# Infini-attention and GELU FFN on one core: four-head score visits, resident attention weights, one ring of PSUM banks, FFN in column halves, transposes by DMA

## The chip, the cores and the metric

The kernel runs on one core of a Trainium2 chip. TensorE does matmuls (PE in the profile; PEld is its load of the stationary operand), VectorE (DVE) and ScalarE (ACT) work elementwise and may read PSUM, where matmul results land, GpSimd (POOL) works elementwise on SBUF, and SyncE (SP) issues the DMAs. The metric is device time in microseconds (us): the median of several runs.

## The reference

One transformer layer on x of 2048 x 576, in bfloat16. Attention has 32 heads of 18 columns and goes through four segments of 512 rows. Within a segment it is causal softmax attention; beside it, a memory M, z, made of earlier segments' keys and values, is read by the queries, and a gate per head mixes both. Then follows an FFN of width 4608. Both have a layernorm before and a residual after.

```python
for s in range(N):
    logits = jnp.einsum('bhqd,bhkd->bhqk', qs, ks) * scale + mask
    a_dot = jnp.einsum('bhqk,bhkd->bhqd', _softmax(logits, axis=-1), vs)
    pq = phi(qs)                      # t + 1 where t > 0, else exp(t)
    a_mem = einsum(pq, M) / (einsum(pq, z)[..., None] + 1e-06)
    outs.append(g * a_mem + (1.0 - g) * a_dot)
    M = M + jnp.einsum('bhld,bhle->bhde', phi(ks), vs)
    z = z + jnp.einsum('bhld->bhd', phi(ks))
...
h = x + (o @ wo)                      # o from the layernormed x
h2 = h + gelu(_layernorm(h) @ w1 + b1) @ w2 + b2
```

## The kernel before

A segment s has four tiles of 128 rows and goes through four phases.

*Phase P* makes Q, K and V. Per tile: layernorm (`layernorm`, L175 to L184: statistics on DVE, a power on POOL, one DVE operation); five transposes on TensorE into PSUM (L195) and a copy by ScalarE to `xnT_t` (L66); three projections of ten matmuls each of 288 columns (`proj`, L203 and L205); ScalarE copies Q and K to padded tiles, 32 columns a head (L72); eight more TensorE transposes each for Q and K (L259, L264), which DVE copies to `QT_al_s` and `KT_al_s` (L260, L265); V goes to `v_augs` (L268), and phi(K) is made by ACT, POOL and DVE (L254, L270, L272). After four tiles, 32 small matmuls add up the memory (L281).

*Phase A* is attention, by groups of four heads. The scores come transposed, keys on partitions. There are three steps per group, of 512, 384 + 128 and 256 columns. In each step the four heads' scores go to two PSUM tiles of two banks (`unit2`, pool psS with two buffers; matmuls at L338, one head per 32 rows of TensorE); ScalarE takes the exp of a pair of heads at a time (L347), POOL clears what lies above the diagonal (L349), and TensorE multiplies with V into the bank `ox` (PV, L356), which DVE clears first (L308) and reads at the end (L361 to L371). From the second segment on, phi(Q) is made per group (L312 to L316: e_g on ACT, r_g on POOL, pq on DVE) and multiplied with the memory (L323).

*Phase B* projects the output and adds the residual. Per tile: five TensorE transposes of `o_nat`, copy, `proj` with wo, add of x (L392), layernorm, five transposes into `xn2T_s`; POOL adds b2 (L401) and the sum goes to the DRAM tile `hd` (L402).

*Phase C* is the FFN. F1: nine groups of four column tiles; a group's weights `w1g` are loaded by three DMAs (L410 to L414, two buffers); a column tile is five matmuls of 512 columns (L419, L420) in a bank of psC (three buffers), copied to `hT` by DVE (L424); gelu runs over twelve column tiles at once (L428). F2: per row tile and half of the columns 36 matmuls (L437) add up in a bank; DVE adds `hc`, loaded from `hd` (L432), and the output is stored (L441).

The code is traced as P, A, B of all four segments and then C of all four. A scheduler lays down each engine's order by priority, that is by order of tracing, and lets later work in where earlier work isn't ready. psS serves P, A and B; psC serves C alone. Buffers of a pool are handed out in the order of tracing, and a new user waits until the old one is done. All DMAs are issued on SP's queue, in order. The attention weights go through three buffers and are loaded anew for each segment; w2 is loaded once, in four chunks, behind the first segment's inputs.

Of the kernel before, what the change touches and what calls it, by code (L numbers as in the profile page):

```python
# [8 lines left out]
ACT = mybir.ActivationFunctionType  # L9
# [3 lines left out]
PSUM = bass.MemoryType.PSUM  # L13


@with_exitstack
def kernel(
# [15 lines left out]
    dbg = None  # L33
    nseg_run = None
# [11 lines left out]
    KT = 5  # L46
# [8 lines left out]
    FORCE4 = False  # L55
    HIPRI = True
    GB = 3
    EVAC_ACT = 0
    XT_DVE = False
    QK_DVE = False  # L60

    def copy_xt(out, in_):
        if XT_DVE:
            nc.vector.tensor_copy(out=out, in_=in_)
        else:
            nc.scalar.copy(out=out, in_=in_)  # L66

    def copy_qk(out, in_):
        if QK_DVE:
            nc.vector.tensor_copy(out=out, in_=in_)  # L70
        else:
            nc.scalar.copy(out=out, in_=in_)  # L72
    if nseg_run is None:
        nseg_run = NSEG
    SYNC_DEP = mybir.DependencyInfo(mybir.DependencyClass.Sync, mybir.DependencyReason.DATA)

    const = ctx.enter_context(tc.tile_pool(name="const", bufs=1))
    wpool = ctx.enter_context(tc.tile_pool(name="wpool", bufs=1))
    xpool = ctx.enter_context(tc.tile_pool(name="xpool", bufs=2))
    xtp = ctx.enter_context(tc.tile_pool(name="xtp", bufs=2))  # L80
    xn2Tp = ctx.enter_context(tc.tile_pool(name="xn2Tp", bufs=2))
    tmp1 = ctx.enter_context(tc.tile_pool(name="tmp1", bufs=1))
    alpool = ctx.enter_context(tc.tile_pool(name="alpool", bufs=1))
    ptpool = ctx.enter_context(tc.tile_pool(name="ptpool", bufs=2))
    ptpool1 = ctx.enter_context(tc.tile_pool(name="ptpool1", bufs=1))
    hpool = ctx.enter_context(tc.tile_pool(name="hpool", bufs=2))
    hbpool = ctx.enter_context(tc.tile_pool(name="hbpool", bufs=1))
    small = ctx.enter_context(tc.tile_pool(name="small", bufs=4))
    w1pool = ctx.enter_context(tc.tile_pool(name="w1pool", bufs=2))
    outpool = ctx.enter_context(tc.tile_pool(name="outpool", bufs=2))  # L90
    psS = ctx.enter_context(tc.tile_pool(name="psS", bufs=2, space=PSUM))
# [3 lines left out]
    x_pre = []  # L95
    for tl in range(TPS):
        xt = xpool.tile([P, D], BF16, tag="x", name="xt") if tl < 2 else None
        if xt is not None:
            nc.sync.dma_start(out=xt[:], in_=x[tl * P:(tl + 1) * P, :])
        x_pre.append(xt)  # L100

    def load_w(W, tag):
        wt = wpool.tile([P, KT, D], BF16, tag=tag, name="wt_" + tag)
        nc.sync.dma_start(out=wt[:, 0:4, :], in_=W[0:512, :].rearrange("(k p) n -> p k n", p=P))
        nc.sync.dma_start(out=wt[0:64, 4, :], in_=W[512:576, :])
        nc.gpsimd.memset(wt[64:KTAIL, 4, :], 0.0)
        return wt

    w_pre = {"wq": load_w(A_wq, "wq"), "wk": load_w(A_wk, "wk"), "wvo": load_w(A_wv, "wvo")}
# [28 lines left out]
    for j in range(2):  # L138
        nc.vector.memset(MZ_blk[j][:], 0.0)

    q_pads = [const.tile([P, H, 32], BF16, name=f"q_pad{j}") for j in range(2)]
    k_pads = [const.tile([P, H, 32], BF16, name=f"k_pad{j}") for j in range(2)]
    phik_pads = [const.tile([P, H, 32], BF16, name=f"phik_pad{j}") for j in range(TPS)]
    v_augs = [const.tile([P, H, Dh + 1], BF16, name=f"v_aug{j}") for j in range(TPS)]
    xn_bufs = [const.tile([P, XW], BF16, name=f"xn{j}") for j in range(2)]
    xn2_bufs = [const.tile([P, XW], BF16, name=f"xn2_{j}") for j in range(1)]
    o_nat = const.tile([P, TPS, XW], BF16, name="o_nat")
    for tx in xn_bufs:
        nc.gpsimd.memset(tx[:, D:XW], 0.0)
    for tpad in q_pads + k_pads:  # L150
        nc.gpsimd.memset(tpad[:, :, Dh:32], 0.0)
    for tpad in phik_pads:
        nc.vector.memset(tpad[:, :, Dh:32], 0.0)
    for tv in v_augs:
        nc.vector.memset(tv[:, :, Dh:Dh + 1], 1.0)
    for tx in xn2_bufs:
        nc.gpsimd.memset(tx[:, D:XW], 0.0)
        nc.gpsimd.memset(tx[:, D:D + 1], 1.0)
    nc.gpsimd.memset(o_nat[:, :, D:XW], 0.0)

    hd = tc.dram_tile([S, D], F32, name="hd")
    hT = const.tile([P, NF, L], BF16, name="hT")
    w2_sb = const.tile([P, NF, D], BF16, name="w2_sb")
    w2v = B_w2.rearrange("(f p) d -> p f d", p=P)
    late = {"x_last": None, "w2_last": None}

    def issue_w2():
        for c in range(4):
            d = nc.sync.dma_start(out=w2_sb[:, c * 9:(c + 1) * 9, :], in_=w2v[:, c * 9:(c + 1) * 9, :])
            if late["x_last"] is not None:  # L170
                tc.add_manual_dep(d.ins, late["x_last"].ins.name, SYNC_DEP, reason="bulk FFN weights after the first segment's inputs")
            late["w2_last"] = d

# [12 lines left out]
    def unit2():  # L186
        return psS.tile([P, 2, 512], F32, tag="st2", name="u2")

    def bf16v(bank_ap):
        return bank_ap.bitcast(BF16)  # L190

    def transposes5(src, bank_ap):
        pt = bf16v(bank_ap)[:, 0:KT * P].rearrange("p (k q) -> p k q", q=P)
        for k in range(KT):
            nc.tensor.transpose(out=pt[:, k, :], in_=src[:, k * P:(k + 1) * P], identity=ident[:])  # L195
        return pt

    def proj(xT_t, wt):
        u = unit2()
        for hf in range(2):  # L200
            ps = u[:, hf, :]
            for k in range(4):
                nc.tensor.matmul(out=ps[:, 0:HALF], lhsT=xT_t[:, k, :], rhs=wt[:, k, hf * HALF:(hf + 1) * HALF],  # L203
                                 start=(k == 0), stop=False)
            nc.tensor.matmul(out=ps[:, 0:HALF], lhsT=xT_t[0:KTAIL, 4, :], rhs=wt[0:KTAIL, 4, hf * HALF:(hf + 1) * HALF],  # L205
                             start=False, stop=True)
        return u

    def hview(u):
        return u[:, :, 0:HALF].rearrange("p b (h d) -> p b h d", d=Dh)  # L210

    def pad_view(tpad):
        return tpad[:, :, 0:Dh].rearrange("p (b h) d -> p b h d", b=2)

    st_P = {}
    st_B = {}

    def phase_P(s):
        if s == 0:
            wq_t, wk_t, wv_t = w_pre["wq"], w_pre["wk"], w_pre["wvo"]  # L220
        else:
            wq_t = load_w(A_wq, "wq")
            wk_t = load_w(A_wk, "wk")
            wv_t = load_w(A_wv, "wvo")
        QT_al_s = alpool.tile([P, G, L], BF16, tag="qt", name="QT_al_s")
        KT_al_s = alpool.tile([P, G, L], BF16, tag="kt", name="KT_al_s")
        for tl in range(TPS):
            t = s * TPS + tl
            cols = slice(tl * P, (tl + 1) * P)
            if s == 0 and x_pre[tl] is not None:  # L230
                xt = x_pre[tl]
            else:
                xt = xpool.tile([P, D], BF16, tag="x", name="xt")
                xd = nc.sync.dma_start(out=xt[:], in_=x[t * P:(t + 1) * P, :])
                if s == 0:
                    late["x_last"] = xd
                    if tl == TPS - 1:
                        issue_w2()
            xn = xn_bufs[tl % 2]
            layernorm(xt[:], xn)  # L240
            u0 = unit2()
            pt = transposes5(xn, u0[:, 0, :])
            xnT_t = xtp.tile([P, KT, P], BF16, tag="xnT", name="xnT_t")
            copy_xt(xnT_t[:], pt)
            uq = proj(xnT_t, wq_t)
            q_pad = q_pads[tl % 2]
            copy_qk(pad_view(q_pad), hview(uq))
            if dbg is not None and "q" in dbg:
                nc.sync.dma_start(out=dbg["q"][t * P:(t + 1) * P, :].rearrange("p (h d) -> p h d", d=Dh), in_=q_pad[:, :, 0:Dh])
            uk = proj(xnT_t, wk_t)  # L250
            k_pad = k_pads[tl % 2]
            copy_qk(pad_view(k_pad), hview(uk))
            ek = tmp1.tile([P, H, Dh], BF16, tag="e", name="ek")
            nc.scalar.activation(out=ek[:].rearrange("p (b h) d -> p b h d", b=2), in_=hview(uk), func=ACT.Exp)  # L254
            ut = unit2()
            ptq = bf16v(ut[:, 0, :]).rearrange("p (g q) -> p g q", q=P)
            q2d = q_pad[:].rearrange("p h d -> p (h d)")
            for g in range(G):
                nc.tensor.transpose(out=ptq[:, g, :], in_=q2d[:, g * P:(g + 1) * P], identity=ident[:])  # L259
            nc.vector.tensor_copy(out=QT_al_s[:, :, cols], in_=ptq)  # L260
            ptk = bf16v(ut[:, 1, :]).rearrange("p (g q) -> p g q", q=P)
            k2d = k_pad[:].rearrange("p h d -> p (h d)")
            for g in range(G):
                nc.tensor.transpose(out=ptk[:, g, :], in_=k2d[:, g * P:(g + 1) * P], identity=ident[:])  # L264
            nc.vector.tensor_scalar(out=KT_al_s[:, :, cols], in0=ptk, scalar1=maskcol[:], scalar2=None, op0=ALU.mult)  # L265
            uv = proj(xnT_t, wv_t)
            v_aug = v_augs[tl]
            nc.vector.tensor_copy(out=pad_view(v_aug), in_=hview(uv))  # L268
            rk = tmp1.tile([P, H, Dh], BF16, tag="r", name="rk")
# [228 lines left out]
```

## Time and profile before

The runs took 619.56 us in the median (619.19 to 621.7). One execution was profiled:

| | us | share of the span |
|---|---|---|
| span | 618.1 | |
| PE busy, 4992 matmuls | 553.5 | 90% |
| PEld busy | 331.1 | 54% |
| DVE busy | 327.6 | 53% |
| ACT busy | 319.4 | 52% |
| POOL busy | 154.1 | 25% |
| DMA queue of SP, share of 16 engines | | 29.3% |

The mean granted TensorE clock is 0.939 of full speed. The page cuts the span into 40 slices of 15.45 us and gives the busy share of each in tenths. A line of single instructions has start, duration, engine, line, operation, output <- inputs, shape and count; where the engine stood idle before, what released it stands in brackets. A row of a stretch has the busy time and number of instructions of PE, PEld, DVE, ACT and POOL, the granted clock, the busy share of the DMA engines and their GB/s.

### The profile page before, as it was taken

The numbers are of one execution on the slowest core, as the hardware profiler recorded it, in microseconds if no ns is written. First come the engines' busy times: TensorE is split into PE (matmuls) and PEld (weight loads), VectorE is DVE, ScalarE is ACT, GpSimd is POOL, SyncE is SP. The second block draws the span as 40 slices with busy tenths as digits, with TensorE's granted clock in tenths as the row PEclk, the third lists the DMA queues.
The fourth block names the chain that finished last, engine by engine and source line by source line (L and its number), as shares of the span: only waits on it lengthen the run. The fifth ranks groups of instructions, "written<-read, shape, count | busy, mean of one in ns | idle before, by whom it ended". The sixth has DMA issues, their size and how long they took to land. (4 is left out here: it accounts for less than half of the span.)

```text
span 618.1 us, 12146 instructions
## 1 busy us (share of the span) xinstructions
PE 553.5 (90%) x4992; PEld 331.1 (54%) x4992; DVE 327.6 (53%) x811; ACT 319.4 (52%) x342; POOL 154.1 (25%) x247
## 2 busy tenths in 40 slices
PE   2778875599999998999999998899999999999997
PEld 1553333375444566675444466665544567744576
DVE  5443223467777635647786735555687641166310
ACT  1449951134999931338788742368767540024300
POOL 3124432313342223224323123135331210000000
PEclk9995555599999999999999999999999999999999
DMA  7960003325223113322132333111124432144020
GB/s 194 351 201 3 2 1 97 110 65 147 65 79 110 45 59 123 104 75 85 43 89 67 114 117 117 58 45 30 31 78 116 109 123 77 38 135 129 25 58 20
DMA packets 48223, 54.65 MB, mean 88 GB/s; under 512 B 3204, under 2 KB 44072, under 8 KB 48168
## 3 DMA queue, kind: packets, MB, share of 16 engines
q1 hardware_dynamic: 48168, 53.88, 29.3%
q8 instruction: 39, 0.64, 0.4%
q14 instruction: 16, 0.13, 0.1%
HBM read 46.79 MB, written 7.08 MB: 87 GB/s over the span
## 5 line engine op out<-in xcount | busy, mean ns | idle before, releaser
L437 PEld LDWEIGHTS <-hT 128*128 128x128 bf16 x1152 | 107.5, 98 | 30.3 <-issue 3.5
L428 ACT ACTIVATE hT<-hT 128x6144 bf16<-128x6144 bf16 x12 | 63.9, 5324 | 55.8 <-DVE hT L424 55.7
L419 PEld LDWEIGHTS <-w1g 128*128 128x128 bf16 x576 | 51.3, 98 | 56.0 <-issue 7.4
L203 PEld LDWEIGHTS <-xnT_t 128*128 128x128 bf16 x384 | 36.7, 100 | 24.3 <-ACT xnT_t L66 13.4
L338 PEld LDWEIGHTS <-KT_al_s 32*128 32x128 bf16 x512 | 21.0, 93 | 50.9 <-issue 47.9
L401 POOL TENSOR_TENSOR hb<-h_t,b_bc 128x576 f32<-128x576 f32 x16 | 20.4, 1277 | 76.2 <-DVE h_t L392 76.2
L182 POOL TENSOR_TENSOR rstd<-rstd,mhalf 128x1 f32<-128x1 f32 x32 | 17.5, 549 | 40.3 <-DVE rstd L181 40.3
L314 POOL TENSOR_SCALAR r_g<-QT_al_s 128x512 bf16<-128x512 bf16 x24 | 14.7, 612 | 36.1 <-DVE pq L316 33.4
L420 PEld LDWEIGHTS <-w1g 65*128 65x128 bf16 x144 | 14.0, 97 | 14.4 <-issue 0.6
L312 ACT ACTIVATE e_g<-QT_al_s 128x512 bf16<-128x512 bf16 x24 | 15.1, 630 | 11.4 <-DVE pq L316 8.0
L203 PEld LDWEIGHTS <-oT_t 128*128 128x128 bf16 x128 | 13.6, 109 | 11.0 <-issue 4.2
L316 DVE SCALAR_TENSOR_TENSOR pq<-e_g,r_g 128x512 bf16<-128x512 bf16 x24 | 19.2, 801 | 0.3
L195 PEld LDWEIGHTS <-xn_0_167 128*128 128x128 bf16 x80 | 5.2, 107 | 22.5 <-DVE xn_0_167 L183 21.6
L308 DVE MEMSET ox<- 128x456 f32 x32 | 14.0, 438 | 3.6 <-DVE o_nat L365 1.4
L177 DVE BATCH_NORM_STATS2 stats<-xt 128x6 f32<-128x288 bf16 x32 | 13.5, 441 | 3.9 <-DMA xt<-in_A_x_dram 3.8
L183 DVE TENSOR_SCALAR xn_0_167<-h_t,mv,rstd 128x576 bf16<-128x576 f32 x16 | 9.3, 579 | 9.9 <-POOL rstd L182 9.9
L323 PEld LDWEIGHTS <-pq 128*128 128x128 bf16 x96 | 8.1, 97 | 11.9 <-issue 5.6
L177 DVE BATCH_NORM_STATS2 stats<-h_t 128x6 f32<-128x288 f32 x32 | 13.1, 451 | 0.4
L270 POOL TENSOR_SCALAR rk<-k_pad_155 128x576 bf16<-128x576 bf16 x8 | 5.4, 678 | 28.0 <-ACT k_pad_155 L72 28.0
L205 PEld LDWEIGHTS <-xnT_t 65*128 65x128 bf16 x96 | 9.7, 101 | 2.8
L270 POOL TENSOR_SCALAR rk<-k_pad_156 128x576 bf16<-128x576 bf16 x8 | 5.3, 666 | 21.9 <-ACT k_pad_156 L72 21.2
L428 ACT ACT_TABLE_LOAD x8 | 10.3, 1283 | 0.1
(1911 smaller groups left out, 1416.8 us busy)
## 6 DMA issues: line engine op xcount, KB each, us to landing
w1g<-in_B_w_dram SPq DMA_DIRECT2D x36, 512.0 KB
w_sb<-in_B_w_dram SPq DMA_DIRECT2D x4, 1296.0 KB
hd<-hb SPq DMA_DIRECT2D x16, 288.0 KB
hc<-hd SPq DMA_DIRECT2D x16, 288.0 KB
xt<-in_A_x_dram SPq DMA_DIRECT2D x16, 144.0 KB
wt_wq<-in_A_wq_dram SPq DMA_DIRECT2D x4, 576.0 KB
wt_wk<-in_A_wk_dram SPq DMA_DIRECT2D x4, 576.0 KB
wt_wvo<-in_A_wv_dram SPq DMA_DIRECT2D x4, 576.0 KB
```

Source lines behind the costliest of these rows:

```text
L177: nc.vector.bn_stats(out=stats[:, c, :], in_=src[:, c * HALF:(c + 1) * HALF])
L182: nc.gpsimd.tensor_tensor(out=rstd[:], in0=rstd[:], in1=mhalf[:], op=ALU.pow)
L203: nc.tensor.matmul(out=ps[:, 0:HALF], lhsT=xT_t[:, k, :], rhs=wt[:, k, hf * HALF:(hf + 1) * HALF], start=(k == 0), stop=False)
L308: nc.vector.memset(ox[:, 0:456], 0.0)
L312: nc.scalar.activation(out=e_g[:], in_=QT_al_s[:, g, :], func=ACT.Exp)
L314: nc.gpsimd.tensor_scalar(out=r_g[:], in0=QT_al_s[:, g, :], scalar1=BIG, scalar2=0.0, op0=ALU.min, op1=ALU.max)
L316: nc.vector.scalar_tensor_tensor(out=pq[:], in0=e_g[:], scalar=1.0, in1=r_g[:], op0=ALU.min, op1=ALU.add)
L338: mm = nc.tensor.matmul(out=sts[i // 2][:, i % 2, off:off + n], lhsT=KT_al_s[rows, g, kt * P:(kt + 1) * P], rhs=QT_al_s[rows, g, kt * P:L] ...
L401: nc.gpsimd.tensor_tensor(out=hb[:], in0=h_t[:], in1=b2_bc[:], op=ALU.add)
L419: nc.tensor.matmul(out=ps[:], lhsT=w1g[:, k, j * P:(j + 1) * P], rhs=xn2T_s[:, k, :], start=(k == 0), stop=False)
L428: nc.scalar.activation(out=hT[:, f0:f1, :], in_=hT[:, f0:f1, :], func=ACT.Gelu_apprx_tanh)
L437: nc.tensor.matmul(out=ps[:, 0:HALF], lhsT=hT[:, f, tl * P:(tl + 1) * P], rhs=w2_sb[:, f, hf * HALF:(hf + 1) * HALF], start=(f == 0), stop ...
```

## The change

It rewrites the kernel around five things.

- *Transposes by DMA.* All transposes (xn, Q, K, o_nat, xn2) become DMAs from SBUF to SBUF on SP's queue. The TensorE version stays in the code behind a constant. KT is no longer multiplied with a mask; the pads it would clear hold zeros.
- *Score visits.* One score tile of four banks, a single buffer, takes all four heads of a step. The scores are held in program order, and the masked probabilities go through three buffers. The first PV matmul of a group clears `ox` in place of a memset. The memory read of a group takes one bank instead of two halves in `ox`.
- *One ring of banks.* Projections, memory and FFN all take single banks from psC, three in all, and copy each half out by itself.
- *Held data.* Attention weights stay in SBUF, wo too. Q, K and V have two buffers, for two segments; phi(K) overwrites K's padded tile. xnT and oT have one buffer. POOL adds b2 in place.
- *FFN in two column halves.* hT holds 18 column tiles. Each half runs F1 in six groups of three column tiles, gelu over nine at once, and F2 over 18 matmuls per bank; the first half's sum goes to a second DRAM copy of `hd` and is added in the second half. C of segment s-1 is traced after P, A, B of segment s; P, A and B get a higher priority by as much as the C traced before them.

```diff
+XBAR = True
+RUN_AHEAD = 2
...
-    xtp = ctx.enter_context(tc.tile_pool(name="xtp", bufs=2))
...
+    xtp = ctx.enter_context(tc.tile_pool(name="xtp", bufs=1))
+    qkp = ctx.enter_context(tc.tile_pool(name="qkp", bufs=RUN_AHEAD))
+    vp = ctx.enter_context(tc.tile_pool(name="vp", bufs=RUN_AHEAD))
...
-    psS = ctx.enter_context(tc.tile_pool(name="psS", bufs=2, space=PSUM))
+    psS = ctx.enter_context(tc.tile_pool(name="psS", bufs=1, space=PSUM))
     psX = ctx.enter_context(tc.tile_pool(name="psX", bufs=1, space=PSUM))
     psC = ctx.enter_context(tc.tile_pool(name="psC", bufs=3, space=PSUM))
...
-    def unit2():
-        return psS.tile([P, 2, 512], F32, tag="st2", name="u2")
...
+    def bank(name):
+        return psC.tile([P, 512], F32, tag="c", name=name)
+
+    def transposed(dst, src, nblk, evac, behind=None):
+
+        if XBAR:
+            nc.sync.dma_start_transpose(out=dst, in_=src)
+            return
...
+    def proj(xT_t, wt, evac, behind=None):
+
         for hf in range(2):
+            ps = bank("ps_pr")
...
+            evac(hf, ps[:, 0:HALF])
...
     def phase_P(s):
+        behind = last_pv.get(s - RUN_AHEAD)
...
+            xnT = xtp.tile([P, KT, P], BF16, tag="xnT", name="xnT")
+            transposed(xnT[:], xn[:], KT, "act")
...
+            proj(xnT, w_q, lambda hf, ps: nc.scalar.copy(out=q_pad[:, half(hf), 0:Dh], in_=heads(ps)), behind)
...
+            transposed(QT[:, :, cols], q_pad[:].rearrange("p h d -> p (h d)"), G, "dve")
+            transposed(KT_[:, :, cols], k_pad[:].rearrange("p h d -> p (h d)"), G, "dve")
...
+                st = psS.tile([P, 4, 512], F32, tag="st", name="st")
+                with tc.high_priority():
...
+                            if last_st["mm"] is not None:
+                                tc.add_manual_dep(sm.ins, last_st["mm"].ins.name, ORDER, reason="scores in program order")
...
+                            mm = nc.tensor.matmul(out=o_ps[:, qt, i, :], lhsT=pt_[:, i, blk:blk + P],
+                                                  rhs=vs[kt][:, 4 * g + i, :], start=(head is None), stop=False,
+                                                  skip_group_check=True)
...
+            transposed(oT[:], o_nat[:, tl, :], KT, "act", behind)
...
+            transposed(xn2T[:, :, tl * P:(tl + 1) * P], xn2[:], KT, "act")
+            nc.gpsimd.tensor_tensor(out=h_t[:], in0=h_t[:], in1=b2_bc[:], op=ALU.add)
+            nc.sync.dma_start(out=hd[0, t * P:(t + 1) * P, :], in_=h_t[:])
...
+        for hh in range(2):
+            for fg in range(NH // WF):
...
+                    ps = bank("ps_f1")
...
+                hc = hpool.tile([P, D], F32, tag="hc", name="hc")
+                nc.sync.dma_start(out=hc[:], in_=hd[hh, rows, :])
...
+                if hh == 0:
+                    nc.sync.dma_start(out=hd[1, rows, :], in_=hc[:])
...
-        for s in range(n):
-            phase_P(s)
-            phase_A(s)
-            phase_B(s)
-        for s in range(n):
-            phase_C(s)
...
+    for s in range(NSEG + 2):
+        if s < NSEG:
+            with tc.high_priority(offset=traced_c):
+                qkv = phase_P(s)
+                phase_A(s, *qkv)
+                xs.append(phase_B(s))
+        if s >= 1 and s - 1 < NSEG:
+            at = tc.cur_priority
+            phase_C(s - 1, xs[s - 1])
+            traced_c += tc.cur_priority - at
```

## The prediction

> **What bounds the kernel now.** I read the slices of the span first, then busy times by stretch, then single stretches in order of time. The profiled execution spans 618.1 us; the runs' median is 619.56, so 1.5 us lie around it.
>
> ```profile
> span 618.1 us, 12146 instructions
> ...
> PE   2778875599999998999999998899999999999997
> ...
> ACT  1449951134999931338788742368767540024300
> ...
> PEclk9995555599999999999999999999999999999999
> ```
>
> A slice is 15.45 us. TensorE is full from slice 8 to the end, at the whole clock; only in slices 3 to 7 is it granted half. By stretch (us, then busy time and instructions of PE, weight load, DVE, ACT, POOL, then clock):
>
> ```profile
> 47.47:90.30 42.83, 34.82 (x429) 16.26 (x429) 11.62 (x37) 37.83 (x47) 18.90 (x31) 0.51 0.01 2
> 90.30:118.10 27.80, 13.59 (x69) 8.11 (x66) 10.81 (x28) 4.15 (x6) 7.78 (x9) 0.50 0.31 99
> ...
> 154.00:212.00 58.00, 57.34 (x580) 25.94 (x577) 41.73 (x117) 55.22 (x56) 21.20 (x34) 1.00 0.28 82
> ```
>
> The first row is the attention of segment 0 with nothing beside it: ScalarE is busy 37.83 of 42.83 us, the clock is half. The second is phase B of segment 0, a chain in which TensorE idles half the time. The third is attention of segment 1 with FFN matmuls of segment 0 between its score visits: both engines full, whole clock. So from 119 us on the kernel is bound by TensorE's work, and only because the FFN, with PSUM banks of its own (psC), fills every hole of attention.
>
> **The change: order.** All matmul banks but scores and ox now come from one ring of three (psC, taken by `bank`), handed out in the order in which the code is traced. C(s-1) is traced after P, A and B of segment s, so its first bank waits for theirs; P(s+1) comes after C(s-1). The built program's order on TensorE agrees: P0 A0 B0 P1 A1 B1 C0 P2 A2 B2 C1 P3 A3 B3 C2 C3, and no FFN matmul stands between the first and the last score visit of any segment. The covers that are gone: FFN over A1 to A3 and over the B and P chains. I sum the stages one after the other.
>
> **A.** Single instructions of A0 before (start, duration):
>
> ```profile
> 60.06 1.02 ACT L347 ACTIVATE pt_803<-u_797 128x1024 bf16<-128x1024 f32 x1
> ...
> 60.98 1.02 ACT L347 ACTIVATE pt_803<-u_798 128x1024 bf16<-128x1024 f32 x1
> ...
> 64.11 0.39 PE L338 MATMUL u_855<-QT_al_s,KT_al_s 32*128 32x256 bf16 x2
> ...
> 64.55 0.60 ACT L347 ACTIVATE pt_860<-u_855 128x512 bf16<-128x512 f32 x1
> 64.61 0.61 PE L338 MATMUL u_878<-QT_al_s,KT_al_s 32*128 32x512 bf16 x2
> ...
> 65.25 1.02 ACT L347 ACTIVATE pt_884<-u_878 128x1024 bf16<-128x1024 f32 x1
> ```
>
> A pair of wide exps takes 1.94 us (60.06 to 62.00), the narrow pair 1.19 (63.96 to 65.15): 1.94 + 1.94 + 1.19 = 5.07 per group, and the groups repeat every 5.19, because one pair's scores are made while the other's exps run. After, one score tile holds all four heads in all four banks (psS, bufs=1), so the next scores wait for both exps. ScalarE then idles from an exp's end to the score (0.09, 64.02 to 64.11) plus score to exp (0.64 wide, 64.61 to 65.25; 0.44 narrow): 0.73 + 0.73 + 0.53 = 1.99. A group is 7.06, A0 8 x 7.06 + 2.5 of edges = 59 us. Whole clock would halve the score part: at 46.05 to 46.55 such a four-head visit left 0.55 idle; 6.6 per group. I take half, as this row of before is the nearest and the new one idles more. For s > 0, e_g (0.63, ACT) fits the holes, r_g (0.61, POOL) can push a mask: plus 0.4, A = 62. What is queued behind the waiting score on TensorE is PV of the step before, then the next scores; PV's masks are ready by then (two selects 1.22 + PV 0.7 against a narrow step of 1.7), so it adds nothing. The ox memsets that go (0.44 each) lay on DVE beside ScalarE's exps: nothing; uncovered they would have been 3.5 us per A.
>
> **The transposes.** Removed: 496 on TensorE, 8 in 0.61 us at the whole clock, and their copies out of PSUM. Added: 80 DMAs on SP's queue, of 5 or 8 blocks of 128x128, 21 blocks per tile in P and 10 in B.
>
> ```profile
> 25.16 0.61 PE L259 MATMUL u_313<-ident,q_pad_154 128*128 128x128 bf16 x8
> ...
> 569.47 0.38 SPq L410 DMA_DIRECT2D w1g<-in_B_w_dram  x1
> ...
> 574.46 1.04 PE L419 MATMUL ps_f_7519<-xn2T_s,w1g 128*128 128x512 bf16 x4 [0.56 <-DMA w1g<-in_B_w_dram]
> ...
> DMA packets 543, 0.52 MB, mean 261 GB/s; under 512 B 33, under 2 KB 543, under 8 KB 543
> ...
> q1 hardware_dynamic: 543, 0.52, 76.0%
> ```
>
> No transposing DMA is in the trace. Around the data I take 1.5 us from w1g's load: 1.05 from issue to the first data, 0.45 from the last (about 574.0) to the matmul. The last two lines are 545 to 547 us: 76% of 16 engines for 2 us over 543 packets is 45 ns for a row of 1024 bytes. A block is 128 rows of 256 bytes, 8 per engine. Low end, cost by bytes: 32 KB at the 357 GB/s of 20 to 30 us, r = 0.09 us per block. Middle, a packet's 45 ns for each row: 0.36. High, 45 ns for each 64 bytes, the row length of beta's load: 1.44. I take 0.36, the packet being what the trace shows rows to cost; estimate T5 = 1.5 + 5r = 3.3 us, T8 = 4.4.
>
> The Trainium skill holds both ends. "VectorE: DVE Perf Modes", section The three transpose paths, gives 390 ns on TensorE and 1309 ns by DMA for 128x128, and its rules take TensorE where PSUM will do. The trace's 76 ns on TensorE is far below the page's, which speaks against the change more strongly still; 1309 ns per block would make the total below an estimated 1270 us. "Advanced Engine Details and Errata", section X-Bar Transpose (TRN2), says such DMAs are as fast as regular ones, which is the low end.
>
> **P.** xnT has one buffer, so tile t+1's transpose waits for V's projection of t; on SP it stands behind QT(t) and KT(t), which wait for ScalarE's copies; PE's next projections wait for it. From xnT's landing, at half clock (five matmuls each 1.20 us apart at 13.91 and 15.11): Q 2.4, copy 0.6, issue to data 1.05, then 21 blocks in a row, 0.45: 4.5 + 21 x 0.36 = 12.1 us per tile against 6.8 before (22.68 to 29.50). Four: 48 us. P0 starts at 16 (before 12.7: the transpose queues behind 0.65 MB of w_o, and the transpose takes the place of a copy). The w2 chunks (3.7 us each) stream while Q is projected: nothing, or 15 us in P0 without that cover. For P2 and P3 tile 0 lies under C: 42 each. Resident weights drop 24 load issues; before they ran ahead under FFN matmuls, so nothing is gained (a 648 KB load is 1.9 us at 357 GB/s). The phi of K, now in place, waits for KT's DMA and leads the first scores by 1.5 us, which is in the 12.1 of the last tile (KT lands at 10.3).
>
> **B.** oT (T5 3.3), projection 2.6 (89.40 to 91.99), 0.3: 6.2 per tile, 25 us; hd(t) waits for POOL's add, and oT(t+2) is behind it on SP, 4.4 + 3.3 + 2.9 for two tiles, less than 12.4. B0 is followed by layernorm 2.9, xn2T and P1's xnT 3.3 + 1.8: 8 us. Later tails lie under C.
>
> **C.** Rows of the tail before:
>
> ```profile
> 540.93 1.03 PE L419 MATMUL ps_f_7275<-xn2T_s,w1g 128*128 128x512 bf16 x4
> ...
> 542.01 1.03 PE L419 MATMUL ps_f_7282<-xn2T_s,w1g 128*128 128x512 bf16 x4
> ...
> 601.47 4.57 PE L437 MATMUL ps_f_7749<-w_sb,hT 128*128 128x288 bf16 x36
> ...
> 605.88 4.57 PE L437 MATMUL ps_f_7791<-w_sb,hT 128*128 128x288 bf16 x36
> ```
>
> An F1 column tile is 1.08 us, 36 F2 matmuls 4.41. Half: 18 x 1.08 = 19.5; F2 17.6; w1g groups of 3 columns last 3.25 against a reload of about 3.8, 0.3 x 4 = 1.2; after the last F1, copy 0.9 and gelu (5.32 x 4608/6144 = 4.0), less 27 F2 matmuls that run first (3.3): 1.8; 0.2. Sum 40.3, C = 81 (before 74.3 of pure work). The 32 more hd transfers (288 KB) lie under F2, a tile of which lasts 4.4 us; a w1g load caught behind one would stall F1 by about 1 us. DVE's 32 more F2 adds (0.46) lie there too.
>
> **Sum.** 16 + P0 48 + A0 59 + B0 25 + 8 + P1 48 + A1 62 + B1 25 + C0 81 + (P 42 + A 62 + B 25 + C 81) x 2 + C3 81 + last add and store 3 = 876; plus 1.5: about 878. With r = 0.09 a P tile is bound by projections, 7.3 + 1.95 = 9.2: 15 x 2.9 + 16 x 1.35 off, 813. Each 0.1 of r above costs (15 x 21 + 16 x 5 + 15) x 0.1 = 41: r = 1.44 gives 1321.
>
> **Rivals.** *Transposes bound it* (r about 1): P tiles of 25 us; 1140 at r = 1, 1321 at the high end. For it: 496 blocks through one queue, in chains; against: the queues move 357 GB/s when full. *Cheap transposes and the whole clock* in P, A and B: P tile 3.65 + 1.95 = 5.6, group 6.6, B tile 4: 16 + 25 + 55 + 16 + 5 + 22 + 58 + 16 + 81 + (18 + 58 + 16 + 81) x 2 + 81 + 3 = 724, 726 with what lies around. For it: P0 before keeps the clock at 76% busy; against: A0 and B0 lost it. *Not slower*: the FFN does hide behind attention, as before, so the change doesn't serialize; place, the holes of A1 to A3 with their P; price, three C of 81 off: 878 - 243 = 635 at r = 0.36, 570 at 0.09; it beats 619.56 from r = 0.32 down. The 57.34 of 58 us above shows that such filling works; against it is the order on TensorE, which is fixed when the program is built.
>
> **How the numbers follow.** Serial order with r from 0.1 to 0.7: 0.72, its own range 800 to 1020; transposes bound 0.13; cheap and whole clock 0.12; not slower 0.03. The prediction is 878 us. The range leaves out part of both slower rivals: 780 to 1110. 0.5% is about what a measurement can tell from no change; faster by more 0.02, within 0.01, slower 0.97.
>
> **What would show it.** In the profile after: no FFN line within an attention stretch; ScalarE idle about 0.7 us before each first exp, released by PE; groups every 7 us; xnT's landing as releaser of the first Q matmul, tiles every 12 us; C of 81 us at whole clock; half clock elsewhere. FFN rows in A1, or P tiles of 25 us, or a span under 780 would prove me wrong.

## The result, and the profile after

The changed kernel takes 823.7 us (median; 822.63 to 826.82) against 619.38 for the kernel before on the same chip: ratio 1.328, 95% interval 1.324 to 1.332. The prediction was 878, range 780 to 1110. The profiled execution spans 821.1 us.

The head and the slices of the page after; a slice is now 20.5 us:

```profile
span 821.1 us, 11325 instructions
...
PE   1544433665437898956444889876544689999997
...
ACT  1326630247640302227761120313875011112121
...
PEclk9975555775556999986555899997555599999999
```

TensorE has four valleys of 3 to 5 tenths where before it had one. They are P, A and B of each segment; ScalarE peaks in them, and the granted clock falls to half. The hills between are FFN alone. By stretch (columns as before) A0, B0, A1 and C3:

```profile
55.80:115.40 59.60, 27.55 (x477) 16.70 (x474) 11.80 (x36) 39.69 (x48) 21.20 (x36) 0.55 0.03 6
115.40:144.00 28.60, 10.32 (x40) 5.33 (x40) 15.40 (x42) 0.00 (x0) 8.85 (x11) 0.50 0.52 124
...
176.70:239.00 62.30, 30.13 (x506) 18.37 (x506) 27.06 (x75) 45.34 (x57) 26.34 (x44) 0.53 0.02 5
...
737.00:818.00 81.00, 75.66 (x470) 44.87 (x467) 32.38 (x53) 16.17 (x4) 0.00 (x0) 1.00 0.34 103
```

The third row answers to before's 154 to 212: there TensorE ran 580 matmuls of attention and FFN in 58 us, here 506 of attention alone in 62.3, at a clock of 0.53. The first FFN matmul stands at 258.8 us (before: 119.8). The FFN's matmuls alone (tile `ps_f`, busy tenths in the same slices) leave out every A:

```profile
busy tenths in 40 slices 0000000000006999900000999990000299999999
```

A group of A0, one row for each pair of exps and the scores before the second:

```profile
71.28 1.94 ACT L304 ACTIVATE pt<-st 128x1024 bf16<-128x1024 f32 x2 [0.77 <-POOL pt L307]
...
73.27 0.62 PE L297 MATMUL st<-QT,KT 32*128 32x384 bf16 x8 [1.57 <-ACT pt L304]
...
74.01 1.94 ACT L304 ACTIVATE pt<-st 128x1024 bf16<-128x1024 f32 x2 [0.80 <-POOL pt L307]
76.51 1.08 ACT L304 ACTIVATE pt<-st 128x512 bf16<-128x512 f32 x2 [0.56 <-PE st L297]
78.37 1.94 ACT L304 ACTIVATE pt<-st 128x1024 bf16<-128x1024 f32 x2 [0.78 <-POOL pt L307]
```

The exps end at 73.22, the scores that waited for them run from 73.27 to 73.89, the next exps start at 74.01. The bracket names POOL, but POOL's mask of that time starts only at 73.33, on the exps just ended; the scores came last. The period is 78.37 - 71.28 = 7.09 us.

Transposes, in P1 (SPq is SP's queue: start of the issue and how long SP takes for it):

```profile
147.10 1.24 SPq L168 DMA_TRANSPOSE QT<-q_pad  x1
...
149.50 1.23 SPq L168 DMA_TRANSPOSE KT<-k_pad  x1
...
150.53 0.29 PE L189 MATMUL ps_pr<-w_v,xnT 65*128 65x288 bf16 x1
...
150.85 1.22 SPq L168 DMA_TRANSPOSE xnT<-xn  x1
...
152.84 0.76 DVE L237 SCALAR_TENSOR_TENSOR k_pad<-ek,rk 128x576 bf16<-128x576 bf16 x1 [1.53 <-DMA KT<-k_pad]
...
153.52 1.14 PE L185 MATMUL ps_pr<-w_q,xnT 128*128 128x288 bf16 x4 [2.70 <-DMA xnT<-xn]
```

xnT goes out when V's projection ends and its reader starts 2.67 us later; the DVE operation that waits for KT (it overwrites `k_pad`, KT's source) starts 3.34 us after KT's issue. KT has eight blocks of 128x128, xnT five; three blocks more cost 0.67, which makes 0.22 us per block and 1.55 around them. The tile lasts from 144.06 to 153.52, 9.46 us.

The stages, by the edges of the trace:

| stage | predicted | measured |
|---|---|---|
| start, end | 19 | 19.8 |
| P0, P1, rest of P2, rest of P3 | 48, 48, 42, 42 | 39.3, 32.7, 24.4, 24.7 |
| A0 to A3 | 59, 62, 62, 62 | 59.6, 62.3, 62.4, 61.4 |
| B0 to B3 | 25 each | 20.9, 19.7, 19.7, 20.7 |
| B0 to P1 | 8 | 7.8 |
| C0 to C3 | 81 each | 90.5, 90.4, 84.1, 80.8 |
| sum | 876 | 821.2 |

### The profile page after: what moved, and what is told of

The parts are those of the page before. It is cut to its first block, busy times and chain, and to the rows that moved or that the text cites. A ratio compares the mean times of both kernels' runs of the same rounds, so it can differ in the third digit from the quotient of the medians.

```text
span 821.1 us, 11325 instructions
## 1 busy us (share of the span) xinstructions
PE 549.0 (67%) x4496; PEld 329.2 (40%) x4496; DVE 306.1 (37%) x701; ACT 279.3 (34%) x316; POOL 152.7 (19%) x251
## 5 line engine op out<-in xcount | busy, mean ns | idle before, releaser
L304 ACT ACTIVATE pt<-st 128x1024 bf16<-128x1024 f32 (+1 forms) x192 | 158.7, 878 | 61.2 <-POOL pt L307 38.9
L383 ACT ACTIVATE hT<-hT 128x4608 bf16<-128x4608 bf16 x16 | 64.7, 4043 | 294.3 <-DVE hT L379 294.3
L376 PE MATMUL ps_f<-xn2T,w1g 128*128 128x512 bf16 x576 | 152.9, 388 | 14.7 <-DMA w1g<-in_B_w_dram 13.6
L394 PE MATMUL ps_f<-w_sb,hT 128*128 128x288 bf16 x1152 | 144.8, 286 | 13.0 <-ACT hT L383 11.9
L379 DVE CAST hT<-ps_f 128x512 bf16<-128x512 f32 x144 | 99.2, 690 | 72.0 <-PE ps_f L377 71.7
L297 PE MATMUL st<-QT,KT 32*128 32x128 bf16 (+3 forms) x512 | 50.7, 433 | 82.0 <-ACT pt L304 81.1
L307 POOL TENSOR_SCALAR_AFFINE_SELECT pt<-pt 128x512 bf16<-128x512 bf16 x128 | 83.2, 662 | 115.6 <-ACT pt L304 62.2
L376 PEld LDWEIGHTS <-w1g 128*128 128x128 bf16 x576 | 55.2, 99 | 90.5 <-DMA w1g<-in_B_w_dram 25.7
L316 PE MATMUL ox<-v_aug,pt 128*128 128x19 bf16 x1280 | 56.3, 181 | 28.9 <-POOL pt L307 19.7
L316 PEld LDWEIGHTS <-pt 128*128 128x128 bf16 x1280 | 44.1, 105 | 69.4 <-POOL pt L307 69.4
L377 PE MATMUL ps_f<-xn2T,w1g 65*128 65x512 bf16 x144 | 56.0, 389 | 0.8 <-DMA w1g<-in_B_w_dram 0.8
```

What stands on the lines that cost most here:

```text
L297: sm = nc.tensor.matmul(out=st[:, i, off:off + n], lhsT=KT_[rows, g, kt * P:(kt + 1) * P], rhs=QT[rows, g, kt * P:L], start=True, stop=Tru ...
L304: nc.scalar.activation(out=pt_[:, 2 * hp:2 * hp + 2, 0:W], in_=st[:, 2 * hp:2 * hp + 2, 0:W], func=ACT.Exp, scale=scale)
L307: nc.gpsimd.affine_select(out=pt_[:, :, off:off + P], in_=pt_[:, :, off:off + P], pattern=[[0, 4], [1, P]], compare_op=ALU.is_ge, fill=0.0 ...
L316: mm = nc.tensor.matmul(out=o_ps[:, qt, i, :], lhsT=pt_[:, i, blk:blk + P], rhs=vs[kt][:, 4 * g + i, :], start=(head is None), stop=False, ...
L376: nc.tensor.matmul(out=ps[:], lhsT=w1g[:, k, j * P:(j + 1) * P], rhs=xn2T[:, k, :], start=(k == 0), stop=False)
L377: mm = nc.tensor.matmul(out=ps[:], lhsT=w1g[0:KTAIL, 4, j * P:(j + 1) * P], rhs=xn2T[0:KTAIL, 4, :], start=False, stop=True)
```

## Experiments

The question is how the 204 us divide, and above all whether the shared ring makes the stages serial. Every kernel was timed beside the kernel before (619.5 to 621.2 us).

**e1, two rings.** The only edit:

```diff
-    psC = ctx.enter_context(tc.tile_pool(name="psC", bufs=3, space=PSUM))
+    psC = ctx.enter_context(tc.tile_pool(name="psC", bufs=2, space=PSUM))
+    psD = ctx.enter_context(tc.tile_pool(name="psD", bufs=1, space=PSUM))
...
+        if name in ("ps_f1", "ps_f2"):
+            return psC.tile([P, 512], F32, tag="c", name=name)
+        return psD.tile([P, 512], F32, tag="d", name=name)
```

> The changed kernel with its three shared banks divided: two for the FFN, one for projections, memory sums and memory reads. Nothing else differs. Theory (one ring handed out in tracing order serializes the stages): the FFN of a segment fills the holes of the next segment's P and A again; P0, A0 and B0 still run alone until about 136 us (plus some 10 us, since one bank makes each projection half wait for the copy of the one before), and what is left is about the 499 us that the kernel before needs after its B0, less the transposes that are gone from TensorE (372 x 0.076 = 28 us): 600 to 680 us, likeliest 620. FFN matmuls stand between the score visits of segments 1 to 3, and the clock is whole there. Rival (the transposes by DMA and their chain on SP's queue set the time): no gain, over 780. Rival (the four-head visits set it): A stays at 62 us each even with FFN in it, and only P and B hide something: 720 to 780.

723.5 us (721.05 to 724.37): 100 us less than the changed kernel, and 44 above the theory's range. That is the time which the second rival gave, but not its sign: A1, with FFN in it, lasts 82 us and not 62. Its stretches of early A1, late A1 and B1:

```profile
208.00:250.00 42.00, 39.40 (x384) 23.05 (x385) 25.46 (x57) 25.95 (x28) 10.53 (x17) 1.00 0.35 103
250.00:292.00 42.00, 31.44 (x444) 22.18 (x441) 16.65 (x48) 31.35 (x35) 16.21 (x26) 0.88 0.14 40
292.00:324.00 32.00, 11.69 (x47) 5.28 (x43) 16.74 (x46) 0.00 (x0) 8.87 (x12) 0.50 0.46 112
```

The serial order is broken: in early A1 FFN matmuls stand between the score visits and the clock is whole. But FFN of segment 0 ends at 277 us; A1's tail then runs alone at a clock of 0.63, and B1 at 0.50. One cause for its being used up so early is taken up at e10.

**e2, transposes on TensorE** (`XBAR = False`, nothing else).

> The changed kernel with its transposes back on TensorE (the constant turned off); one ring, four-head visits and all else as changed. Theory (the ring's order costs most, the transposes little): P tiles go from 8.8 to 10.5 us to about 7, B tiles from 5.25 to about 6.5, so 13 x -2.5 + 16 x 1.3 = -12: 800 to 830 us, likeliest 812. Rival (the transposes by DMA cost the bulk of the 204 us): under 720.

807.1 us (803.45 to 807.28): 17 us less than the changed kernel. P0 takes 24.6 instead of 39.3 us, B0 24.8 instead of 20.9. The DMAs cost little here, and in B they even gain.

**e3, score pairs.**

```diff
-    psS = ctx.enter_context(tc.tile_pool(name="psS", bufs=1, space=PSUM))
+    psS = ctx.enter_context(tc.tile_pool(name="psS", bufs=2, space=PSUM))
...
-                st = psS.tile([P, 4, 512], F32, tag="st", name="st")
+                sts = [psS.tile([P, 2, 512], F32, tag="st", name="st") for _ in range(2)]
```

> The changed kernel with its score tile of four banks divided into two tiles of two banks, two buffers, each for a pair of heads, as before; one ring and transposes by DMA as changed. Theory (a single score buffer makes ScalarE wait out each score visit): a group goes from 7.09 to about 5.2 us, 32 groups x 1.9 = 60 us less: 755 to 775. Rival (POOL's masks or PV, which the profile names as releasers of 38.9 us of ScalarE's waits, hold the group): a group stays near 7 us, 810 to 825.

766.6 us (764.41 to 768.55): 57 us less than the changed kernel. ScalarE in A0:

```profile
67.66 4.98 ACT L305 ACTIVATE pt<-st 128x1024 bf16<-128x1024 f32 x6 [0.27 <-PE st L298]
72.81 4.97 ACT L305 ACTIVATE pt<-st 128x1024 bf16<-128x1024 f32 x6 [0.17 <-PE st L298]
77.94 2.99 ACT L305 ACTIVATE pt<-st 128x1024 bf16<-128x1024 f32 x3 [0.16 <-PE st L298]
```

Six exps, which are one group, stand in a row; then comes a gap of 0.17. A group takes 5.15 us. The wait of the single buffer is shown to be worth 57 us; masks and PV, unchanged here, don't hold the group at 7 us.

**e4, e1 and e2 together.**

> Two rings as in e1 and transposes on TensorE as in e2. Theory: with the FFN beside attention TensorE is the bound, and 372 transposes after B0 add 28 us and their copies to it, P0 and B0 gain or lose under 10: e1 plus 10 to 35 us, 630 to 700. Rival (transposes by DMA hold up the chain on SP's queue behind the loads of FFN weights): faster than e1 by 10 us or more.

768.3 us (764.89 to 769.41): 45 above e1, where I had expected 10 to 35. P1 takes 59 instead of 52 us and B1 30 instead of 21: transposes and projections now share one bank. In P0, which has no FFN beside it, the trace shows TensorE waiting 0.5 to 0.8 us for the copy out of that bank before nearly each of them. So e2 and e4 differ in sign; what a transpose on TensorE costs depends on the banks it gets.

**e5, PSUM as before.** Projections, memory sums and scores in two tiles of two banks, two banks for the FFN, one for the memory read:

```diff
+    def unit2(name):
+        return psS.tile([P, 2, 512], F32, tag="st", name=name)
...
-            ps = bank("ps_pr")
+            ps = u[:, hf, :]
...
-                om = bank("ps_om")[:, 0:4 * 76]
+                om = psO.tile([P, 512], F32, tag="om", name="ps_om")[:, 0:4 * 76]
```

> The changed kernel with PSUM laid out much as before: four banks as two tiles of two for scores, projections and memory sums, one for ox, two for the FFN alone, one for the memory read. Transposes by DMA, held weights, FFN in halves and the order of tracing stay as changed. Theory (the 204 us are the sum of: one ring, four-head visits, and little else): the attention chain gets as short as before (P 40, A 60, B 25 us with FFN in the holes), and TensorE's work sets the time, 28 us of transposes less and some 25 us of stalls at FFN weights and gelu more: 615 to 660 us, likeliest 635. Rival (transposes by DMA and FFN halves carry a cost of their own that e1 showed, since it stayed at 723): 680 or more. Rival (without the PSUM changes the rest is a gain): under 605.

696.8 us (695.11 to 700.28); the first rival's number. Again A1 is long (88 us) and B1 alone:

```profile
184.00:272.00 88.00, 79.20 (x823) 46.52 (x822) 42.52 (x103) 57.37 (x62) 25.91 (x44) 0.96 0.22 67
272.00:302.00 30.00, 10.96 (x40) 5.15 (x40) 15.48 (x43) 0.00 (x0) 8.42 (x11) 0.50 0.48 112
```

With ring and visits undone, 77 us are still missing; my theory that these two are nearly all of the loss falls here.

**e6, the kernel before with DMA transposes,** such as:

```diff
-            pt = transposes5(o_nat[:, tl, :], ub[:, 0, :])
-            copy_xt(oT_t[:], pt)
+            nc.sync.dma_start_transpose(out=oT_t[:], in_=o_nat[:, tl, :])
```

> The kernel before with all 80 transposes as DMAs on SP's queue and nothing else changed (the mask of KT, whose pads are zero, goes with the copy). Theory (transposes by DMA cost a lone chain little and take 372 x 0.076 = 28 us of work off TensorE where it is the bound): P0 some 9 us longer, B0 some 6 shorter, 28 off the rest: 585 to 625 us, likeliest 600. Rival (a transposing DMA waits at the head of SP's queue for its input and holds up the FFN and attention weights behind it): 640 or more.

627.8 us (621.0 to 630.17), ratio 1.010 (1.006 to 1.014): 3 above the theory's range, and well below the rival's 640. TensorE's busy time falls from 553.5 to 524.6, the time doesn't. In P0 an xnT stands behind two chunks of w2, and TensorE waits 17 us for it:

```profile
32.08 1.28 SPq L169 DMA_DIRECT2D w_sb<-in_B_w_dram  x2
33.47 5.81 SPq L243 DMA_TRANSPOSE xnT_t<-xn  x1
...
44.35 1.14 PE L203 MATMUL u<-wt_wq,xnT_t 128*128 128x288 bf16 x4 [17.04 <-DMA xnT_t<-xn]
```

**e7, the kernel before with one ring** (`bank()` hands out one psC buffer, and each half is copied out by itself, as in the changed kernel), and **e8, with e7's order of tracing alone:**

```diff
-        u = unit2()
+        u = [bank(), bank()]
...
-    mode = "attn_first"
+    mode = "lag1"
```

> The kernel before with transposes, projections and memory sums moved to the FFN's ring of three banks, and C of segment s-1 traced after P, A and B of segment s as in the changed kernel (with C at the end two xn2T buffers would not do). Score pairs, TensorE transposes, FFN in one piece and reloaded weights stay. Theory (the ring alone serializes): P0 A0 B0 118, three times P 30 + A 46 + B 28 = 312, four C of 75 = 300, less some 15 where a first P tile or a B tail lies under C: 700 to 745 us, likeliest 717; no FFN in the stretches of A. Rival (the ring is harmless, the wait comes from elsewhere): within 10 us of before.

> The kernel before with nothing but the order of tracing of e7 (C of segment s-1 after P, A and B of s). It tells the order of tracing from the ring. Theory: the banks stay apart, so FFN work still fills the holes: 610 to 640. Rival (the order of tracing serializes by itself): 690 or more, near e7.

e7: 764.7 us (763.35 to 765.89). e8, which has the second edit only: 620.5 (619.28 to 621.08), ratio 1.001 (0.999 to 1.003). The same stretch, A1, and behind it the FFN's matmuls by slices, first in e7, then in e8:

```profile
135.00:195.00 60.00, 39.94 (x529) 21.29 (x526) 35.71 (x116) 44.06 (x57) 25.50 (x42) 0.57 0.11 34
...
busy tenths in 40 slices 0000000000019999000000999900000299999999
```

```profile
148.00:221.00 73.00, 71.94 (x741) 35.30 (x739) 50.64 (x145) 66.44 (x64) 24.91 (x40) 1.00 0.27 82
...
busy tenths in 40 slices 0000000154999999946899899954899999999999
```

e7 runs attention alone at a clock of 0.57, e8 fills it. The ring by itself makes a serial order and costs 145 us; the order of tracing costs nothing. e7 is 48 above my 717 and 20 above the range: A1 to A3 alone last 56 to 59 us, not 46, because memory read and PV share ox (ScalarE idles 1.22 us per group there, released by PV), and C is 78 rather than 75.

**e9 and e10: e5 with the FFN in one piece, then also with TensorE transposes.**

```diff
-RUN_AHEAD = 2
+RUN_AHEAD = 1
...
-    hT = const.tile([P, NF // 2, L], BF16, name="hT")
+    hT = const.tile([P, NF, L], BF16, name="hT")
...
-    NH = NF // 2
-    WF = 3
+    NH = NF
+    WF = 4
```

> e5 with the FFN in one piece, as before: hT of 36 column tiles, nine groups of four, F2 over 36 matmuls per bank, no second hd copy (Q, K and V get one buffer to make room, as before). Theory (the halves cost e5 its last 75 us in part: four C of 81 instead of 74, and C of segment s-1 is used up before B of s, which then runs alone): 650 to 675, likeliest 665. Rival (what is left lies in P and B with transposes by DMA alone): within 10 us of e5's 697.

> e9 with its transposes back on TensorE. What is left of the change is held attention weights, half-wise copies, the memory read in a bank of its own (two for the FFN), ox without memsets, and the order of tracing with raised priorities. Theory (transposes by DMA lengthen P from 28 to about 40 us a segment, 3 x 10 on a chain that sets the pace): 615 to 645, likeliest 630. Rival (the chain isn't the bound, TensorE's work is): 10 to 30 us slower than e9.

e9: 688.4 us (683.25 to 691.12), 8 us less than e5, the rival's number. The halves, and the second buffer of Q, K and V that went with them, are worth no more than that here. e10: 664.8 (663.49 to 668.18), 24 less than e9, above its range. TensorE in P1 of e10:

```profile
130.78 0.29 PE L190 MATMUL ps_pr<-w_q,xnT 128*128 128x288 bf16 x1
130.91 0.38 PE L383 MATMUL ps_f<-xn2T,w1g 128*128 128x512 bf16 x1
131.12 0.28 PE L190 MATMUL ps_pr<-w_q,xnT 128*128 128x288 bf16 x1
131.24 0.38 PE L383 MATMUL ps_f<-xn2T,w1g 128*128 128x512 bf16 x1
```

Projection and FFN alternate one for one. FFN is no filler here but a rival on a level with attention: P1 lasts 64.5 us, and C0 is used up at 240, before B1. In the kernel before, a projection's five matmuls stand together. The cause is in the code: leaving `high_priority(offset=traced_c)` puts the priority counter back. It stands at 58 when P1 is traced, and at 58 again when C0 begins, though P1, A1 and B1 lie between. e12 tests this. e1 and e5 raise priorities in the same way; whether that alone is what they lack was not tried.

**e11, e6 for segments 1 to 3 only** (`if s > 0`).

> e6 with the transposes of segment 0 back on TensorE, so that none waits behind a chunk of w2; segments 1 to 3 keep theirs as DMAs. Theory (e6 lost up to 17 us in P0 where xnT stood behind w2 on SP's queue, and gains a little later from 372 transposes less on TensorE): 600 to 618, faster than before by 0 to 3%. Rival (e6's loss lies in the later segments, at transposes behind weight loads): 622 or more.

625.0 us (619.07 to 626.97), ratio 1.005 (1.001 to 1.008): not the gain I expected, but the rival's number. P0 is mended. From 119 to 616 us TensorE's busy time falls from 477.6 to 461.5 and its idle time grows by as much. The stretch around B2 shows where; first e11, then the kernel before:

```profile
328.00:357.00 29.00, 20.54 (x118) 9.85 (x114) 20.84 (x51) 5.32 (x1) 9.11 (x11) 0.93 0.79 193
```

```profile
344.00:383.00 39.00, 35.21 (x301) 23.79 (x299) 20.46 (x51) 17.52 (x14) 9.03 (x11) 1.00 0.39 121
```

TensorE is busy for 71% of it, before for 90%. The largest single wait of e11 there is for a load of FFN weights:

```profile
339.96 0.45 SPq L423 DMA_DIRECT2D w1g<-in_B_w_dram  x1
...
345.52 1.20 SPq L409 DMA_TRANSPOSE xn2T_s<-xn  x1
...
349.47 0.47 SPq L426 DMA_DIRECT2D w1g<-in_B_w_dram  x1
...
351.94 0.28 SPq L427 DMA_DIRECT2D w1g<-in_B_b_dram  x1
...
353.99 1.44 PE L433 MATMUL ps_f<-xn2T_s,w1g 65*128 65x512 bf16 x3 [5.50 <-DMA w1g<-in_B_b_dram]
```

The three loads of one group of weights, which the kernel before issues within 1 us, lie 12 us apart here, because B2's transposes and stores, which wait for their inputs, stand between them on SP's queue. This is the mechanism that e6's rival named, seen at one place. Over the whole span TensorE also waits 6.5 us for xnT and 5.7 for oT, in 13 waits of at most 3.1 us.

**e12, e10 with plain priorities.**

```diff
-            with tc.high_priority(offset=traced_c):
-                qkv = phase_P(s)
-                phase_A(s, *qkv)
-                xs.append(phase_B(s))
+            qkv = phase_P(s)
+            phase_A(s, *qkv)
+            xs.append(phase_B(s))
```

> e10 without the raised priorities: P, A and B are traced plainly, C of segment s-1 after P, A and B of s as before. Leaving the raising puts the count of priorities back to where it stood (segment 0's C starts at 58, as P1 does), so that in e10 the FFN of a segment stands on a level with the attention it should fill: matmuls of P1 and F1 alternate, P1 lasts 64 us, and C0 is used up before B1, which runs alone. Theory (this costs e10 its last 43 us): P1 back to about 30 us, FFN beside B1: 612 to 632, likeliest 620. Rival (two FFN banks instead of three and the bank for the memory read cost it): 650 or more.

635.7 us (635.13 to 643.49), 29 less than e10, 4 above my range, ratio to before 1.027 (1.023 to 1.031). B1 and the chain around it in e10, then in e12:

```profile
264.00:295.00 31.00, 15.10 (x72) 8.20 (x72) 12.25 (x31) 4.55 (x7) 5.47 (x6) 0.50 0.19 63
```

```profile
230.00:260.00 30.00, 27.36 (x229) 20.08 (x227) 13.69 (x40) 9.06 (x8) 5.50 (x7) 1.00 0.25 79
```

P1 is back at 32 us and B1 is filled. The last 15 us lie among what is left of the change (held weights, half-wise copies, two banks for the FFN and one for the memory read, `ox` without memsets); they were not told apart. No version beat the kernel before.

## Why the prediction was right

The time fell within the range, on the right side and for the reason given, 54 us below the likeliest value. By its steps:

- *Order.* Right, and shown: no FFN matmul lies in any A, the ring alone serializes (e7, with e8 as control), and with the ring parted the FFN runs beside attention again (e1).
- *A.* Right to 1 us in the sum: 245.7 against 245. A group is 7.09 (7.06), idle 0.77, 0.80, 0.56 (0.73, 0.73, 0.53); pairs give back 57 us (e3).
- *Transposes.* The fixed 1.5 was right (1.55); the block was mis-sized, 0.22 us and not 0.36. T5 is 2.67 (3.3), T8 3.34 (4.4). The Trainium skill, "VectorE: DVE Perf Modes", section The three transpose paths, gives 1309 ns for a 128x128 transpose by DMA. Taken for each block, as the prediction tried it, that doesn't hold here: five blocks in one DMA took 2.67 us in all.
- *P.* The step "21 blocks in a row" failed. QT and KT lie beside the projections; SP is free again 0.12 us before xnT can go. A tile is its three projections plus T5, 6.8 + 2.7 = 9.5 at half clock, which is the form I had kept for cheap transposes. The clock also comes back within P (0.78 in the later tiles of P1), which I had not expected. P is 121 us in place of 180: the whole of the 54 and more.
- *w2 under the Q projection: "nothing".* Wrong: a chunk went out at 40.97, xnT behind it at 42.63, and its reader waited 9.59 us where 2.7 to 3.3 was usual in P1: 6 to 7 us.
- *B.* 5.25 us per tile (6.2), the 0.6 of T5 and 0.3 of slack: 81 in place of 100.
- *C.* C3, alone, is 80.8 (81). C0 and C1 are 90: B's last tile and the first of P lie in them, as I said, but on TensorE, which is full there; I had counted them as free. Their matmuls take 5.2 of C0's 9.7 us above C3; another 2.9 are FFN matmuls that are slower in C0, at a clock of 0.79 in its first 9 us. The sum had 22 us too little here.
- *Rivals.* Transposes as the bound: fell (e2, 17 us). Cheap transposes and whole clock: the first half came true in part, the second only in part of P. FFN behind attention: fell by the trace. The 635 it would have brought were too low as well: e1, where FFN does run beside attention, took 723.5. That the freed FFN competes on equal priority there is shown for e10 (by e12), not for e1.

The parts don't add up to 204, since they hide one another: the ring alone costs 145 (e7), taking it away from the changed kernel gives 100 (e1). One way through, from after to before: pairs 57, ring 70 (e3 to e5, with a bank for the memory read and two for the FFN), halves 8, DMA transposes 24, priorities 29, rest 15. In another order the shares would differ.

## What to carry to other kernels

A shared pool is an order: buffers go out as the code is traced, and late filler work that takes them can't start early (145 us in e7). Look, for each piece of work meant to fill holes, at every pool it takes from, and read the built order of the bound engine. Where a filler does run, see that it ranks below what it fills; one that ranks equal is used up early and leaves the next hole empty.

## What the runs showed of the hardware

- A transposing DMA took 2.67 us from issue to reader for 128 x 640 and 3.34 for 128 x 1024 with no bulk load just ahead on the queue (P1 of the changed kernel); behind chunks of w2 6.7 (its P0) and 10.9 (e6, issued 33.47, read 44.35). SP is busy 1.2 us with issuing each, 5.81 in that row of e6.
- Taking busy time off TensorE, which was 90% busy, gave nothing (29 us in e6; 16 us of it from 119 us on in e11): it waited instead, for transposing DMAs to land and for a weight load that stood behind them and B's stores.
